# Attention and FFN of the first token group moved ahead of the loads and attention of the second, in a linear-attention kernel with a snake FFN

## The chip, the cores and the metric

The kernel runs on one core of one Trainium2 chip. The metric is device time in microseconds (us) of one execution. A run lists several executions, most of which agree within about 1.5%. The profile is one execution; its span is about 2 us below the time of the same execution. Engines are written PE (TensorE matmul), PEld (TensorE weight load), DVE (VectorE), ACT (ScalarE), POOL (GpSimd) and SP (SyncE, which issues most DMAs). Some matmul records are missing from a trace, a few per cent; the weight loads of the FFN are all there (384 for FFN1, 400 for FFN2), so work is counted by them here.

## The reference

```python
# linear attention with decay, blocks of 64, state kv per (batch, head); q, k, v: [4, 8, 768, 64]
intra = einsum(q_b, k_b) * Dmask ; intra = einsum(intra, v_b)
inter = einsum(q_b * lam_pow, kv_state)
out   = intra + inter
kv_state = lam_block * kv_state + einsum(k_b * rev_pow, v_b)
# then, on x = attention output as [3072, 512]:
h = x @ w_in                          # 512 -> 2048
s = sin(alpha * h)
g = h + s * s / (alpha + 1e-9)
y = g @ w_out                         # 2048 -> 512
```

## The kernel before

Work is cut into 24 attention *units* (256 positions of one batch and four heads) and 6 token *groups* of 512 tokens; group g needs units 4g to 4g+3. The code and the profile count groups from 0; this text says "group one" for g = 0 and "group two" for g = 1. FFN1 has 16 tiles per group (four 128x128x512 matmuls each); FFN2 has four accumulations per group (16 matmuls each).

A unit's loads are three DMAs of 256 KB on the SP queue. The weights are cast from fp32 to bf16 by DMAs that GpSimd issues:

```python
def load(u, after=None):
    for nm, src in (("q", q), ("k", k), ("v", v)):
        ld = nc.sync.dma_start(out=..., in_=...)         # 256 KB; waits for `after` if given
def load_w_in(j):  nc.gpsimd.dma_start(out=w_in_sb[..j..], in_=moe_w_in[..j..])    # 4 chunks
def load_w_out(j): nc.gpsimd.dma_start(out=w_out_sb[..j..], in_=moe_w_out[..j..])  # 4 chunks
```

A unit is scaled (QL, KD), transposed (QT), multiplied to scores, masked, and gives its state; its output needs the state before it:

```python
scores(n)            # PE into PSUM s0, s1
domask(n)            # DVE, frees s0, s1
kvmm(n, okv)         # PE
kv_copy(n, okv)      # ACT
kv_decay(n, 0)       # POOL: add, multiply, multiply (kvx, kvbd, kvs)
intermm, outmm, outev  # PE, PE, ACT: output of the unit before
```

An FFN1 tile holds one PSUM buffer from its first matmul to the end of `gall`:

```python
def fin():                                            # after the four matmuls
    s1 = sin(alpha * hps)                             # ACT
    s2 = s1 * s1                                      # on `sq`: DVE, ACT or POOL
    gall[g][:, f] = s2 * r + hps                      # DVE, then the PSUM buffer is free
```

The order of the kernel before, cut:

```python
for u in range(8): load(u)
busy(N0)                                   # filler matmuls
group(0); group(1)                         # attention of units 0..7; w_in is issued from unit 5 on (WIN0 = 5)
for f in range(16):                        # FFN1 of group one
    run(ffn1(0, f)) ; if f < 4: load_w_out(f)
    if f == GATE: load(8, after=...)       # GATE = 0
# then pairs: two FFN1 tiles of group two, two quarters of FFN2 of group one, with units 8.. between
# steady state: FFN1 tile, FFN2 quarter, alternating, one attention unit per eight of them
```

Of the kernel before, what the change touches and what calls it, by code (L numbers as in the profile page):

```python
# [12 lines left out]
BF16 = mybir.dt.bfloat16  # L13
# [4 lines left out]
def kernel(  # L18
# [23 lines left out]
    NU = 4 * NG  # L42
    RING = 8
    WIN0 = 5
    GATE = 0
# [54 lines left out]
    for u in range(8):  # L100
        load(u)
# [83 lines left out]
    def transposes(u, tag="s0", split=False):  # L185
        QT = work.tile([P, 2, 2, 2, P], BF16, name="QT")
        if split:
            pts = [ps.tile([P, 2, 2, P], BF16, name="pt", tag=tag, bufs=BUFS[tag])
                   for j in range(2)]
        else:  # L190
            pt = ps.tile([P, 2, 2, 2, P], BF16, name="pt", tag=tag, bufs=BUFS[tag])
            pts = [pt[:, 0], pt[:, 1]]
# [236 lines left out]
    def group(g, tag):  # L429

        n0 = 4 * g
        okv = None
        for n in range(n0, n0 + 4):
            nxt = n + 1 < 8
            if nxt:
                scale_q(n + 1, V)
                scale_k(n + 1, G)
            if n >= WIN0 and n < WIN0 + WCH:
                load_w_in(n - WIN0)
            okv = new_okv()  # L440
            if n > 0:
                intermm(n - 1, okv)
                outmm(n - 1, okv)
            scores(n)
            domask(n)
            kvmm(n, okv)
            kv_copy(n, okv)
            kv_decay(n, 0)
            if n > 0:
                outev(n - 1, okv)  # L450
            if nxt:
                transposes(n + 1, tag, True)
                cast_v(n + 1, A)
            busy(NB)

# [5 lines left out]
    group(0, "hps")  # L461
# [4 lines left out]
    group(1, "hps")  # L466
    for j in range(8 - WIN0, WCH):
        load_w_in(j)
    okv = new_okv()
    intermm(7, okv)  # L470
    outmm(7, okv)
    outev(7, okv)
# [4 lines left out]


    TAGS = ("hps", "s0", "hps", "s1", "hps", "ops")
    SQ = (V, A, V, A, G, A, V, G)  # L480
    for f in range(NFC):
        run(ffn1(*f1q.pop(0), SQ[f % 8], TAGS[f % 6] if f < 15 else "hps"))
        if f < 4:
            load_w_out(f)
        if f == GATE:
            load(8, after=f1mm[0, f])

    def slot(n, out=True):

        okv = new_okv()  # L490
        if out:
            intermm(n - 1, okv)
        if n < NU:
            scores(n)
        if out:
            outmm(n - 1, okv)
        if n < NU:
            kvmm(n, okv)
        if out:
            outev(n - 1, okv)  # L500
        if n < NU:
            domask(n)
            kv_copy(n, okv)
            kv_decay(n, 0)

    def dec(k):
        for _ in range(k):
            if decq and decq[0] in kva:
                kv_decay(decq.pop(0), 1)

    def macro(at, order="12121212", sq=(V,)):


        F1 = [ffn1(*f1q.pop(0), sq[i % len(sq)])
              for i in range(order.count("1")) if f1q]
        F2 = blocks(ffn2(*f2q.pop(0), "hps" if not F1 and len(f2q) % 2 else "ops"), 4)
        for j, x in enumerate(order):
            for do in at.get(j, ()):
                do()
            if x == "1":  # L520
                if F1:
                    run(F1.pop(0))
            else:
                run(F2.pop(0))

    L = lambda f, *a, **k: (lambda: f(*a, **k))


    Fa = blocks(ffn2(*f2q.pop(0)), 4)
    Fb = blocks(ffn2(*f2q.pop(0), "s1"), 4)  # L530

    def pair(k, sq):
        for j in range(2):
            run(ffn1(*f1q.pop(0), sq[j], ("hps", "s0")[j] if k < 3 else "hps"))
        run(Fa[k])
        run(Fb[k])

    scale(8, G, G, A)
    transposes_dma(8)
    pair(0, (V, A))  # L540
    load(9, after=f1mm[1, 1])
    dec(1)
    pair(1, (V, V))
    load(10)
    dec(1)
    pair(2, (V, V))
    scale(9, V, G, A)
    transposes_dma(9)
    load(11)
    pair(3, (V, V))  # L550
    dec(1)
    scale(10, V, G, A)
    transposes_dma(10)
    load(12)
    macro({1: [L(slot, 8, False)],
           3: [L(scale, 11, V, G, A), L(transposes_dma, 11), L(load, 13)],
           5: [L(slot, 9)],
           7: [L(dec, 1)]})
    macro({0: [L(scale, 12, V, G, A), L(transposes_dma, 12), L(load, 14)],
           1: [L(slot, 10)],  # L560
           5: [L(slot, 11)],
           6: [L(scale, 13, G, G, A), L(load, 15)],
           7: [L(dec, 1)]})

    for n in range(12, NU + 8):
        at = {}
        if n <= NU:
            at[0] = [L(slot, n)]
            if n + 1 < NU:
                at[0].append(L(transposes_dma, n + 1))  # L570
            if n + 2 < NU:
                at[0].append(L(scale_q, n + 2, G))
            if 16 <= n + 4 < NU:
                at[0].append(L(load, n + 4))
            at[1] = [L(dec, 2 if n < 17 else 1)]
            if n + 2 < NU:
                at[1] += [L(scale_k, n + 2, G), L(cast_v, n + 2, G)]
        if len(f2q) == 1:
            break
        macro(at, "21212121" if n % 4 == 0 else "11121222" if n == NU + 3 else "12121212")  # L580
# [30 lines left out]
```

## Time and profile before

| | before |
|---|---|
| time, median of the runs beside the changed kernel | 228.82 us (228.03 to 231.39) |
| span of the profiled execution | 227.1 us |
| first FFN1 matmul | 33.0 us |
| last matmul ends | 223.2 us |

The first view is the busy time by stretch of the FFN1 line alone. The columns are the stretch, its length, the busy time of matmuls and of weight loads with their counts, the granted clock, the DMA share and GB/s. The second stretch ends where the 193rd weight load begins, the first of FFN1 tile 49 (48 tiles are done).

```profile
core 0: us, PE busy (x) PEld busy (x), PEclk, DMA share, GB/s
0.00:33.00 33.00, 0.00 (x0) 0.00 (x0) 0.95 0.93 221
33.00:119.00 86.00, 46.07 (x186) 18.55 (x193) 0.98 0.97 197
119.00:223.30 104.30, 48.26 (x184) 18.24 (x192) 1.00 0.40 91
```

No FFN work at all is done in the first 33 us, while the DMA engines move 221 GB/s. The last stretch is TensorE at its pace; these are pieces of its chain of waits (start, length, what):

```profile
135.20 0.86 PE ops L377 x4
136.06 0.86 PE hps L349 x4
...
143.13 0.86 PE ops L377 x4
```

Four matmuls take 0.86 us, 0.216 us each before rounding; 32 of them and one attention unit repeat every 7.93 us (143.13 - 135.20), so a unit takes 7.93 - 32 x 0.216 = 1.02 us of TensorE. With these two numbers the waiting in any stretch can be worked out. From 33.0 to 119.0 us TensorE needed 192 + 132 FFN matmuls (70.0 us) and nine units (9.2 us), 79.2 of 86.0 us: about 6.8 us were lost.

The last view is the DMA queues in two stretches of 4 us, 28 to 32 and 40 to 44 us. The columns are packets, MB written, and the time of the packets as a share of 16 engines (packets overlap in the trace, so it can pass 100%, as the 105.5% below). The queue q0 carries the weights, q1 the unit loads.

```profile
q0 software_dynamic: 675, 0.67, 105.5%
```

```profile
q0 software_dynamic: 577, 0.57, 84.1%
q1 hardware_dynamic: 581, 0.29, 35.5%
```

Alone, the weights move 0.17 MB/us (of bf16; the reads are twice that: of the 27.28 MB that the page has as read from HBM, 18.87 are q, k and v, and 8.4 are left for the 4.19 MB that q0 wrote). With loads beside them they keep 0.143 and the loads get 0.073. Both queues moved the same number of packets (577 and 581); a packet of the weights is about 1.0 KB, one of the loads 0.5 KB, and that is the split of two to one.

### The profile page before, as it was taken

The page shows a single profiled execution, that of the slowest core. Times are in us where ns is not written, and L with a number is a line of the kernel's source. Part 1 is how long each engine was busy: PE and PEld are TensorE (multiplying, and loading weights), DVE is VectorE, ACT ScalarE, POOL GpSimd, SP SyncE. Part 2 cuts the span into 40 slices and gives each one's busy share as a digit, 9 for nine tenths or more (in the row PEclk, how much of TensorE's full clock was granted, in tenths as well). Part 3 has the DMA queues.
Part 4 walks back from the last instruction along what each step waited for, and adds up shares of the span by engine and source line. Part 5 has one row for each costly group of instructions (what it writes and reads, how often), then busy time and mean ns, then how long its engine had stood idle before and what let it go on. Part 6 is the DMA issues. An engine that isn't in the chain of part 4 may idle for free.

```text
span 227.1 us, 5244 instructions
## 1 busy us (share of the span) xinstructions
PE 207.8 (91%) x2054; PEld 108.9 (48%) x2077; DVE 158.3 (70%) x268; ACT 115.7 (51%) x200; POOL 114.0 (50%) x176
## 2 busy tenths in 40 slices
PE   8777679997997779999999999999999999999993
PEld 5465444433444345554554555455455444444452
DVE  3866756988895486798887998867987747667000
ACT  2463659964645345645554554445455535554121
POOL 5665995275635459999999855742611000000000
PEclk9996999999999969999999999999999999999999
DMA  5999599999769999984877777484233022201424
GB/s 149 293 289 274 139 177 185 216 213 168 227 166 171 243 204 299 200 207 95 210 158 173 153 190 180 102 208 62 56 73 68 0 49 46 46 9 40 92 49 92
DMA packets 63849, 33.92 MB, mean 149 GB/s; under 512 B 19648, under 2 KB 60880, under 8 KB 63824
## 3 DMA queue, kind: packets, MB, share of 16 engines
q1 hardware_dynamic: 59488, 29.31, 56.7%
q0 software_dynamic: 4224, 4.19, 11.4%
q8 instruction: 16, 0.26, 0.5%
q10 hardware_dynamic: 112, 0.07, 0.1%
q14 instruction: 9, 0.07, 0.1%
HBM read 27.28 MB, written 6.29 MB: 148 GB/s over the span
## 4 chain that ended last, share of the span: by engine, by line
PE 67%; DMA 11%; SPq 6%; DVE 5%; POOL 4%; issue 2%; ACT 2%; ACTq 0%; POOLq 0%
PE ops L377 32%; PE hps L349 26%; DMA st_v<-in_v_dram 8%; SPq L80 5%; DMA st_k<-in_k_dram 3%; PE sp L226 2%; DVE gall L363 2%; PE okv L320 2%; PE okv L305 2%; POOL KD L169 2%; SPq L209 1%; PE okv L254 1%; DVE QL L160 1%; PE bz L427 1%; PE pt L196 1%
## 5 line engine op out<-in xcount | busy, mean ns | idle before, releaser
L349 PE MATMUL hps<-xt,w_in_sb 128*128 128x512 bf16 x370 | 94.3, 379 | 2.4 <-DVE gall L363 1.5
L377 PE MATMUL ops<-w_out_sb,gall 128*128 128x512 bf16 (+1 forms) x391 | 94.7, 372 | 1.1 <-issue 0.7
L377 PEld LDWEIGHTS <-gall 128*128 128x128 bf16 x400 | 38.7, 98 | 42.9 <-issue 0.5
L349 PEld LDWEIGHTS <-w_in_sb 128*128 128x128 bf16 x384 | 36.8, 98 | 45.8 <-issue 3.0
L169 POOL TENSOR_TENSOR KD<-st_k,R 128x512 bf16<-128x512 f32 x24 | 27.5, 1144 | 13.0 <-DMA st_k<-in_k_dram 8.9
L237 DVE TENSOR_TENSOR ST<-sp,mask 128x512 bf16<-128x512 f32 x48 | 30.8, 683 | 3.3 <-PE sp L226 3.1
L384 ACT COPY ob<-ops 128x512 f32<-128x512 f32 (+1 forms) x25 | 14.2, 569 | 16.3 <-PE ops L377 16.3
L331 ACT CAST xt<-okv 128x512 bf16<-128x512 f32 x24 | 14.1, 586 | 6.7 <-PE okv L254 5.8
L178 ACT CAST VB<-st_v 128x512 bf16<-128x512 f32 x14 | 8.7, 623 | 14.8 <-DMA st_v<-in_v_dram 14.8
L160 POOL TENSOR_TENSOR QL<-st_q,E 128x512 bf16<-128x512 f32 x12 | 12.8, 1070 | 0.0
L427 PE MATMUL bz<-zeros 128*128 128x256 bf16 x60 | 10.6, 332 | 1.1 <-DVE warm L94 1.1
L226 PE MATMUL sp<-QT 64*64 64x128 bf16 x384 | 10.4, 228 | 1.2 <-ACT QT L200 0.7
L160 DVE TENSOR_TENSOR QL<-st_q,E 128x512 bf16<-128x512 f32 x12 | 8.7, 728 | 2.2 <-DMA st_q<-in_q_dram 2.1
L320 PE MATMUL okv<-ST,VB 64*64 64x128 bf16 x384 | 10.2, 226 | 0.0
L226 PEld LDWEIGHTS <-QT 64*64 64x64 bf16 x384 | 6.8, 111 | 3.6 <-issue 0.9
L427 PEld LDWEIGHTS <-zeros 128*128 128x128 bf16 x60 | 6.7, 119 | 2.7 <-DVE warm L94 1.1
L254 PE MATMUL okv<-VB,KD 64*64 64x64 bf16 x320 | 7.4, 198 | 0.1
L320 PEld LDWEIGHTS <-VB 64*64 64x64 bf16 x384 | 7.0, 111 | 1.0 <-issue 0.2
L180 POOL CAST VB<-st_v 128x512 bf16<-128x512 f32 x10 | 6.8, 683 | 0.0
L200 ACT COPY QT<-pt 128x512 bf16<-128x512 bf16 x8 | 4.7, 590 | 3.8 <-issue 1.7
L254 PEld LDWEIGHTS <-KD 64*64 64x64 bf16 x320 | 6.2, 114 | 0.4 <-issue 0.2
L196 PE MATMUL pt<-iden,KD 128*128 128x128 bf16 x32 | 3.4, 232 | 2.9 <-POOL KD L169 2.8
(530 smaller groups left out, 303.7 us busy)
## 6 DMA issues: line engine op xcount, KB each, us to landing
st_q<-in_q_dram SPq DMA_DIRECT2D x24, 256.0 KB, 3.6
st_k<-in_k_dram SPq DMA_DIRECT2D x24, 256.0 KB, 4.1
st_v<-in_v_dram SPq DMA_DIRECT2D x24, 256.0 KB, 4.4
out_dram<-ob SPq DMA_DIRECT2D x46, 128.0 KB, 2.5
w_in_sb<-in_moe_w_in_dram POOLq DMA_DIRECT2D x4, 512.0 KB, 6.6
w_out_sb<-in_moe_w_out_dram POOLq DMA_DIRECT2D x4, 512.0 KB, 15.3
QT<-QL SPq DMA_TRANSPOSE x16, 3.4
QT<-KD SPq DMA_TRANSPOSE x16, 2.6
```

The costliest lines, as they stand in the source:

```text
L80: ld = nc.sync.dma_start(out=tl[:].rearrange("p h two e -> p h (two e)"), in_=src[b, hh * HH:(hh + 1) * HH, tp * W:(tp + 1) * W, :] .rearr ...
L160: eng.tensor_tensor(out=QL[:], in0=stage[u][0][:].rearrange("p h two e -> p two h e"), in1=E[:, :, hs].unsqueeze(3).to_broadcast([P, 2, HH ...
L169: eng.tensor_tensor(out=KD[:], in0=stage[u][1][:].rearrange("p h two e -> p two h e"), in1=R[:, :, hs].unsqueeze(3).to_broadcast([P, 2, HH ...
L226: nc.tensor.matmul(out=sp[hd][half[c], par, hp, :], lhsT=QT[half[hd], 1, par, hp, half[c]], rhs=QT[half[hd], 0, :, hp, half[c]], start=Tru ...
L237: nc.vector.tensor_tensor(out=ST[:, hd], in0=sp[hd][:], in1=mask[:].unsqueeze(2).to_broadcast([P, 2, 2, P]), op=ALU.mult)
L254: nc.tensor.matmul(out=okv[half[hd], c, 2 * P + hp * D:2 * P + (hp + 1) * D], lhsT=KD[half[c], par, h, :], rhs=VB[half[c], par, h, :], sta ...
L320: nc.tensor.matmul(out=okv[half[hd], c, hp * P:(hp + 1) * P], lhsT=VB[half[c], par, 2 * hp + hd, :], rhs=ST[half[c], hd, par, hp, :], star ...
L331: nc.scalar.copy(out=xt[g][:, 2 * hh:2 * hh + 2, bb, :, :].rearrange("p hp c i -> p c hp i"), in_=okv[:, :, 0:2 * P].rearrange("p c (hp i) ...
L349: f1mm[g, f] = nc.tensor.matmul(out=hps, lhsT=w_in_sb[:, c, f * P:(f + 1) * P], rhs=xt[g][:, c].rearrange("p b c i -> p (b c i)"), start=( ...
L377: f2mm[:] = [nc.tensor.matmul(out=ops[:], lhsT=gall[g][:, f, m * P:(m + 1) * P], rhs=w_out_sb[:, f, col], start=(f == 0), stop=(f == NFC - ...
L384: nc.scalar.copy(out=ob[:], in_=ops[:])
L427: nc.tensor.matmul(out=bz[:], lhsT=zeros[:, :P], rhs=zeros[:], start=True, stop=True)
```

## The change

The intent: only units 0 to 3 are loaded and computed before FFN1 of group one, w_in is issued from unit 1 on, and w_out right after. The loads of units 4 to 11 wait for FFN1 tile 9 and so are issued after both weights. Units 4 to 7 run between the quarters of FFN2 of group one, whose four accumulations are all open and advance by chunk of w_out. FFN1 of group two then runs as 16 tiles in a row, with units 8 and 9 inside.

In the cut below, `B(j, m, ...)` runs quarter j of the FFN2 accumulations m; `tr` transposes a unit on TensorE, `att_s` runs its scores and state, `att_o` its output, and `att_so` the scores of one unit with the output of the unit before. `dec` runs the second, late state decay of a unit on GpSimd. `seq` runs a string of FFN1 tiles (1) and FFN2 quarters (2) and puts work before the position named: `slot` is an attention unit, `prep` scales a unit, transposes it by DMA and loads the unit four later.

```diff
-    WIN0 = 5
-    GATE = 0
+    GATE = 9
-    for u in range(8):
+    for u in range(4):
         load(u)
 ...
+    for n in range(4):
+        if n < 3: sqk(n + 1)                      # scale q on DVE, k on POOL
+        if n in (1, 2): load_w_in(n - 1)
+        attend(n, new_okv(), n - 1 if n else None)
+        ...
+    attend(None, new_okv(), 3, False)
+    load_w_in(2); load_w_in(3)
+    for j in range(WCH): load_w_out(j)
 ...
+    SQ0 = (V, A, V, A, V, A, G, V, G, A, V, G, G, V, G, G)
     for f in range(NFC):
-        run(ffn1(*f1q.pop(0), SQ[f % 8], TAGS[f % 6] if f < 15 else "hps"))
-        if f < 4: load_w_out(f)
-        if f == GATE: load(8, after=f1mm[0, f])
+        run(ffn1(*f1q.pop(0), SQ0[f], TAGS[f % 6] if f < 14 else "hps"))
+        if f == GATE:
+            for u in range(4, 8): load(u, after=f1mm[0, f] if u == 4 else None)
+            for u in range(8, 12): load(u)
 ...
+    scale(4, V, V, A)
+    B(0, 0, 1, 2, 3)                              # quarter 0 of accumulations 0..3
+    tr(4); scale(5, V, V, A)
+    B(1, 0); att_s(4); dec(1); B(1, 1, 2, 3)
+    ...                                           # the same for units 5, 6 with quarters 2, 3
+    att_so(6); dec(2); B(3, 1, 2, 3)
+    tr(7); scale(8, V, G, A); transposes_dma(8); load(12)
+    busy(NB); att_so(7); busy(NB); att_o(7)
+    SQ1 = (G, V, G, A)                            # who squares, by tile
+    seq("1" * 16, {2: [L(slot, 8, False), L(prep, 9, V, G, A), L(dec, 1)],
+                   8: [L(slot, 9), L(dec, 1), L(prep, 10, V, G, A)],
+                   14: [L(prep, 11, V, G, A)]}, SQ1, TAGS[:1])   # three PSUM buffers
+    seq("2" * 8, {1: [L(slot, 10), L(dec, 1), L(prep, 12, V, G, A)],
+                  5: [L(slot, 11), L(dec, 1), L(prep, 13, V, G, A)]}, SQ1, tags2=("ops", "hps"))
+    seq("112112112112" * 2, ...units 12 to 16...)
+    ...then "12121212" twelve times, and the rest of FFN2
```

More of the change, by code (lines that the diff above doesn't have):

```diff
@@ L187, in transposes @@
         if split:
-            pts = [ps.tile([P, 2, 2, P], BF16, name="pt", tag=tag, bufs=BUFS[tag])
+            tags = (tag, tag) if isinstance(tag, str) else tag
+            pts = [ps.tile([P, 2, 2, P], BF16, name="pt", tag=tags[j], bufs=BUFS[tags[j]])
                    for j in range(2)]
@@ L427, in busy, with sqk, attend @@
                 nc.tensor.matmul(out=bz[:], lhsT=zeros[:, :P], rhs=zeros[:], start=True, stop=True)
-    def group(g, tag):
-        n0 = 4 * g
-        okv = None
-        for n in range(n0, n0 + 4):
-            nxt = n + 1 < 8
-            if nxt:
-                scale_q(n + 1, V)
-                scale_k(n + 1, G)
-            if n >= WIN0 and n < WIN0 + WCH:
-                load_w_in(n - WIN0)
-            okv = new_okv()
-            if n > 0:
-                intermm(n - 1, okv)
-                outmm(n - 1, okv)
+    def sqk(u):
+        scale_q(u, V)
+        scale_k(u, G)
+    def attend(n, okv, n_out, with_scores=True):
+        if n_out is not None:
+            intermm(n_out, okv)
+            outmm(n_out, okv)
+        if with_scores:
             scores(n)
@@ L448, in group @@
             kv_decay(n, 0)
-            if n > 0:
-                outev(n - 1, okv)
-            if nxt:
-                transposes(n + 1, tag, True)
-                cast_v(n + 1, A)
-            busy(NB)
+        if n_out is not None:
+            outev(n_out, okv)
     busy(N0)
@@ L460 @@
     LHP, LBD = decay_tables()
-    group(0, "hps")
     ap = ps.tile([P, NFC], FP32, name="ap", tag="ops", bufs=1)
@@ L465 @@
     nc.vector.reciprocal(out=r_sb[:], in_=alpha_sb[:])
-    group(1, "hps")
-    for j in range(8 - WIN0, WCH):
-        load_w_in(j)
-    okv = new_okv()
-    intermm(7, okv)
-    outmm(7, okv)
-    outev(7, okv)
+    for n in range(4):
+        if n < 3:
+            sqk(n + 1)
+        if n in (1, 2):
+            load_w_in(n - 1)
+        attend(n, new_okv(), n - 1 if n else None)
+        if n < 3:
+            transposes(n + 1, "hps", True)
+            cast_v(n + 1, A)
+        busy(NB)
+    attend(None, new_okv(), 3, False)
+    load_w_in(2)
+    load_w_in(3)
+    for j in range(WCH):
+        load_w_out(j)
     f1q = [(g, f) for g in range(NG) for f in range(NFC)]
@@ L476, with dec, tr, att_s @@
     decq = list(range(NU))
+    def dec(k):
+        for _ in range(k):
+            if decq and decq[0] in kva:
+                kv_decay(decq.pop(0), 1)
     TAGS = ("hps", "s0", "hps", "s1", "hps", "ops")
-    SQ = (V, A, V, A, G, A, V, G)
+    SQ0 = (V, A, V, A, V, A, G, V, G, A, V, G, G, V, G, G)
     for f in range(NFC):
-        run(ffn1(*f1q.pop(0), SQ[f % 8], TAGS[f % 6] if f < 15 else "hps"))
-        if f < 4:
-            load_w_out(f)
+        run(ffn1(*f1q.pop(0), SQ0[f], TAGS[f % 6] if f < 14 else "hps"))
         if f == GATE:
-            load(8, after=f1mm[0, f])
+            for u in range(4, 8):
+                load(u, after=f1mm[0, f] if u == 4 else None)
+            for u in range(8, 12):
+                load(u)
+    def tr(u):
+        transposes(u, ("s0", "s1"), True)
+    F2 = [[] for _ in range(4)]
+    for m in range(4):
+        st = ffn2(*f2q.pop(0), ("hps", "hps", "hps", "ops")[m])
+        F2[m] = blocks(st, 4)
+    def att_s(n):
+        okv = new_okv()
+        attend(n, okv, None)
+    def att_so(n):
+        okv = new_okv()
+        attend(n, okv, n - 1)
+    def att_o(n):
+        attend(None, new_okv(), n, False)
+    def B(j, *ms):
+        for m in ms:
+            run(F2[m][j])
+    scale(4, V, V, A)
+    B(0, 0, 1, 2, 3)
+    tr(4)
+    scale(5, V, V, A)
+    B(1, 0)
+    att_s(4)
+    dec(1)
+    B(1, 1, 2, 3)
+    tr(5)
+    scale(6, V, V, A)
+    B(2, 0)
+    att_so(5)
+    dec(1)
+    B(2, 1, 2, 3)
+    tr(6)
+    scale(7, V, V, A)
+    B(3, 0)
+    att_so(6)
+    dec(2)
+    B(3, 1, 2, 3)
+    tr(7)
+    scale(8, V, G, A)
+    transposes_dma(8)
+    load(12)
+    busy(NB)
+    att_so(7)
+    busy(NB)
+    att_o(7)
     def slot(n, out=True):
@@ L504, in slot, with prep, seq @@
             kv_decay(n, 0)
-    def dec(k):
-        for _ in range(k):
-            if decq and decq[0] in kva:
-                kv_decay(decq.pop(0), 1)
-    def macro(at, order="12121212", sq=(V,)):
-        F1 = [ffn1(*f1q.pop(0), sq[i % len(sq)])
-              for i in range(order.count("1")) if f1q]
-        F2 = blocks(ffn2(*f2q.pop(0), "hps" if not F1 and len(f2q) % 2 else "ops"), 4)
+    L = lambda f, *a, **k: (lambda: f(*a, **k))
+    def prep(u, *eng):
+        scale(u, *eng)
+        transposes_dma(u)
+        if u + 4 < NU:
+            load(u + 4)
+    def seq(order, at, sq, tags1=("hps",), tags2=("ops",)):
+        n1, n2 = order.count("1"), order.count("2")
+        F1 = [ffn1(*f1q.pop(0), sq[i % len(sq)], tags1[i % len(tags1)]) for i in range(n1)]
+        F2 = []
+        for i in range(n2 // 4):
+            F2 += blocks(ffn2(*f2q.pop(0), tags2[i % len(tags2)]), 4)
         for j, x in enumerate(order):
@@ L519, in macro @@
                 do()
-            if x == "1":
-                if F1:
-                    run(F1.pop(0))
-            else:
-                run(F2.pop(0))
-    L = lambda f, *a, **k: (lambda: f(*a, **k))
-    Fa = blocks(ffn2(*f2q.pop(0)), 4)
-    Fb = blocks(ffn2(*f2q.pop(0), "s1"), 4)
-    def pair(k, sq):
-        for j in range(2):
-            run(ffn1(*f1q.pop(0), sq[j], ("hps", "s0")[j] if k < 3 else "hps"))
-        run(Fa[k])
-        run(Fb[k])
-    scale(8, G, G, A)
-    transposes_dma(8)
@@ L540 @@
-    pair(0, (V, A))
-    load(9, after=f1mm[1, 1])
-    dec(1)
-    pair(1, (V, V))
-    load(10)
-    dec(1)
-    pair(2, (V, V))
-    scale(9, V, G, A)
-    transposes_dma(9)
-    load(11)
-    pair(3, (V, V))
-    dec(1)
-    scale(10, V, G, A)
-    transposes_dma(10)
-    load(12)
-    macro({1: [L(slot, 8, False)],
-           3: [L(scale, 11, V, G, A), L(transposes_dma, 11), L(load, 13)],
-           5: [L(slot, 9)],
-           7: [L(dec, 1)]})
-    macro({0: [L(scale, 12, V, G, A), L(transposes_dma, 12), L(load, 14)],
-           1: [L(slot, 10)],
-           5: [L(slot, 11)],
-           6: [L(scale, 13, G, G, A), L(load, 15)],
-           7: [L(dec, 1)]})
@@ L565 @@
-    for n in range(12, NU + 8):
+            run((F1 if x == "1" else F2).pop(0))
+    SQ1 = (G, V, G, A)
[4 more added lines that the diff above has]
+                  5: [L(slot, 11), L(dec, 1), L(prep, 13, V, G, A)]}, SQ1, tags2=("ops", "hps"))
+    seq("112112112112" * 2,
+        {0: [L(slot, 12), L(dec, 1), L(prep, 14, G, G, A)],
+         5: [L(slot, 13), L(dec, 1), L(prep, 15, G, G, A)],
+         10: [L(slot, 14), L(dec, 1), L(prep, 16, G, G, A)],
+         15: [L(slot, 15), L(dec, 1), L(prep, 17, G, G, A)],
+         20: [L(slot, 16), L(dec, 1), L(prep, 18, G, G, A)]}, (V, V, A, V))
@@ L566 @@
+    for i in range(12):
         at = {}
+        n = 17 + i
         if n <= NU:
-            at[0] = [L(slot, n)]
-            if n + 1 < NU:
-                at[0].append(L(transposes_dma, n + 1))
+            at[1] = [L(slot, n), L(dec, 2)]
             if n + 2 < NU:
-                at[0].append(L(scale_q, n + 2, G))
-            if 16 <= n + 4 < NU:
-                at[0].append(L(load, n + 4))
-            at[1] = [L(dec, 2 if n < 17 else 1)]
-            if n + 2 < NU:
-                at[1] += [L(scale_k, n + 2, G), L(cast_v, n + 2, G)]
@@ L578 @@
-        if len(f2q) == 1:
-            break
-        macro(at, "21212121" if n % 4 == 0 else "11121222" if n == NU + 3 else "12121212")
+                at[1].append(L(prep, n + 2, G, G, G))
+        seq("12121212", at, (V,))
+    for m in range(3):
+        run(ffn2(*f2q.pop(0), "hps" if m % 2 else "ops"))
     run(ffn2(*f2q[0], "ops", slice(0, DM // 2)))
```

## The prediction

> **What bounds the kernel now.** Two stages. From 84 us to the end the chain of waits is TensorE alone: FFN matmuls of 0.216 us (four in 0.864), one attention unit per 7.93 us period, so a unit costs TensorE 7.93 - 32 x 0.216 = 1.02 us. From 33 us the needed TensorE work is 768 x 0.216 = 165.9 us plus 17 units, 183.2 us; the last matmul ends at 223.2 us, so only 7 us is lost after 33 us (timeline: gaps at 52, 56, 72 and 79 us). The first 33 us hold no FFN matmul (stretches of the FFN1 line): eight attention units, one per 2.7 us, run behind 6.3 MB of loads at 285 GB/s, and w_in is issued only at 25 us. The change attacks that head.
>
> **What the change does.** Four units instead of eight precede FFN1; w_in is issued from about 12 us. Before, unit 3's scores were at 16.6 us; now two weight issues (0.8-0.95 us) sit on GpSimd inside the loop. I estimate FFN1 to start at 19.8 us, 13.2 us earlier. Four units (4 x 1.02, and 4 x 0.45 of transposes) move behind it: about 190 us of work. Without any new stall the span would be 19.8 + 190 + 4 = 214.
>
> **New stalls, estimated from traced durations.**
> 1. DMA. Weights alone moved 0.17 MB/us (bf16 written); with loads beside them (40 to 48 us) 0.143, loads 0.073 (DMA view by stretch). [...] So unit 4, gated at FFN1 tile 9 (28 us), lands at 37-40 us, unit 5 at 43-44, w_out at 42. FFN2 of group one reaches unit 4 at 38 us; unit 5's scaling stands on VectorE before unit 4's mask. Loss 3-4 us.
> 2. Hand-over from FFN1 to FFN2, 1 us, and the exposed unit 7 after FFN2, 3 us.
> 3. FFN1 of group two runs as 16 tiles without FFN2 between. VectorE needs 16 x 0.75 + 4 x 0.42 + two masks (2 x 1.29) + three scalings (0.69) = 18.4 us against TensorE's 15.9. Worse, tiles 2 and 8 have their square (1.03 us) on GpSimd behind two decays of 1.46 us and one k scaling of 1.1 us. With three PSUM buffers each costs up to 4 us. Loss 3-8 us. VectorE squares also stretch from 0.42 to 1.24 us beside GpSimd[...].
> 4. The 16 FFN1 with 8 FFN2 quarters: VectorE 5.3 us per five blocks and a slot against TensorE's 5.34: 0-2 us.
>
> The head's 13 us lie fully on the critical path; new losses of 10-18 us replace the old 7. Added in full they give a span near 229; such waits partly overlap, and the hand-set engine lists suggest balancing, so I expect 224.5 span, 226.5 us (times are 2 us above the span).
>
> **Prediction:** 226.5 us, 219 to 234 in 8 of 10; faster by over 2% 0.40, within 2% 0.38, slower 0.22.
>
> **What would show the steps.** First FFN1 matmul at 19-21 us; FFN1 of group one gapless for 14 us; waits of QL and KD for loads of units 4 and 5 at 38-45 us; gaps in FFN1 of group two at tiles 5 and 11, ended by gall; after about 92 us saturated TensorE at 0.216 us.
>
> **What would make it wrong.** Weights later than 20 us; loads keeping less than a third of the DMA beside w_out; GpSimd blocking FFN1 of group two less or more than estimated; a lower granted clock.

VectorE squares in the trace of the kernel before took 0.42 us with no GpSimd instruction beside them and up to 1.24 us with one; the cause was not shown. The sum: 19.8 + 190 + 4 = 214 us without new stalls; the stalls 3-4, 1 + 3, 3-8 and 0-2 us are the 10-18 us; in full that gave a span near 229 us, of which 4.5 were taken off, 224.5, and 226.5 us with the 2 us between time and span.

## The result, and the profile after

| | before | after |
|---|---|---|
| time, median | 228.82 us (228.03 to 231.39) | 248.51 us (246.25 to 249.5) |
| ratio after / before, 95% interval | | 1.0883 (1.0806 to 1.0960) |
| span of the profiled execution | 227.1 us | 247.4 us |
| first FFN1 matmul | 33.0 us | 20.2 us |
| last matmul ends | 223.2 us | 243.5 us |

Ratios are the mean time of one kernel's fast runs over that of the other's of the same rounds, so not quite the ratio of the medians. The same view of the FFN1 line of the changed kernel:

```profile
core 0: us, PE busy (x) PEld busy (x), PEclk, DMA share, GB/s
0.00:20.19 20.19, 0.00 (x0) 0.01 (x1) 0.92 0.94 203
20.19:136.40 116.21, 48.35 (x184) 19.14 (x193) 0.91 0.86 182
136.40:243.60 107.20, 49.00 (x190) 18.78 (x192) 1.00 0.35 79
```

This is the whole ledger. The head is 12.8 us shorter (33.0 to 20.2). The middle, to the same FFN1 tile (49, a point of equal FFN1 work in both kernels), is 30.2 us longer (86.0 to 116.2). The rest is 2.9 us longer (104.2 to 107.1 by the end of the last matmul), of which 0.9 us are four FFN2 matmuls that the middle had not done. The sum is the 20.3 us between the spans. The steady pace is untouched, as two pieces of the chain of waits show:

```profile
139.97 0.86 PE hps L349 x4
140.83 0.86 PE ops L377 x4
```

The middle now needs 192 + 128 FFN matmuls (69.1 us), 13 units (13.3 us), four units' transposes (an estimate of 0.45 us each, as four of the eight take some 0.4 us and overlap) and eight fillers (0.109 us each, by their starts in the trace at full clock, 0.9 us), 85.1 us. So 5.9 us of its 30.2 us is work that moved in, and the waits in it went from 6.8 to 31.1 us. Where they are, the busy time of all engines by stage shows. The stages are FFN1 of group one (20.2 to 35), FFN2 of group one with units 4 to 7 (35 to 67.5), FFN1 of group two (67.5 to 97.2), two accumulations of FFN2 (97.2 to 109.7), and the mixed stage:

```profile
core 0: us, PE busy (x) PEld busy (x) DVE busy (x) ACT busy (x) POOL busy (x), PEclk, DMA share, GB/s
20.20:35.00 14.80, 13.70 (x65) 6.16 (x64) 11.26 (x18) 12.47 (x20) 8.46 (x10) 1.00 1.13 178
35.00:67.50 32.50, 24.18 (x303) 13.51 (x304) 15.85 (x26) 10.72 (x21) 12.94 (x23) 0.85 1.10 252
67.50:97.20 29.70, 20.09 (x149) 8.50 (x149) 15.77 (x24) 14.68 (x25) 16.86 (x22) 0.82 0.40 102
97.20:109.70 12.50, 10.03 (x188) 5.78 (x188) 7.29 (x11) 5.41 (x11) 9.11 (x15) 1.00 0.68 131
109.70:139.40 29.70, 27.11 (x353) 14.41 (x348) 24.82 (x40) 21.68 (x39) 26.15 (x40) 1.00 1.01 210
```

| stage | length | TensorE needs | lost |
|---|---|---|---|
| FFN1 of group one | 14.8 | 13.8 | 1.0 |
| FFN2 of group one, units 4 to 7 | 32.5 | 13.8 + 4.1 + 1.8 + 0.9 = 20.6 | 11.9 |
| FFN1 of group two, units 8, 9 | 29.7 | 13.8 + 2.0 = 15.8 | 13.9 |
| two FFN2 accumulations, units 10, 11 | 12.5 | 6.9 + 2.0 = 8.9 | 3.6 |

In the two bad stages no engine is full: VectorE is busy 15.8 of 29.7 us, ScalarE 14.7, GpSimd 16.9. This is waiting along chains, not a lack of throughput. Also, the granted clock is 0.85 and 0.82 there.

What TensorE waited for in these two stages (the view of waits; the columns are who waited for whom, us in total, how often, the longest), first 35 to 67.5 us, then 67.5 to 97.2 us:

```profile
PE bz L427 <- ACT ob L384: 4.0, 1, 4.0
PE pt L196 <- DVE KD L168: 1.9, 1, 1.9
```

```profile
PE hps L349 <- DVE gall L363: 9.2, 5, 4.9
```

The 9.2 us are waits for a PSUM buffer. The timeline shows what held it, at the first of the two long ones (start, length, engine, line, what, and in brackets the engine's idle time before it and what ended it):

```profile
72.50 1.04 POOL L168 TENSOR_TENSOR KD<-st_k,R 128x512 bf16<-128x512 f32 x1
73.50 0.45 POOL L285 TENSOR_TENSOR kvx<-kva,kvs 128x128 f32<-128x128 f32 x1
74.03 0.61 POOL L288 TENSOR_TENSOR kvbd<-kvx,LBD 128x256 bf16<-128x256 f32 x1
74.60 0.85 POOL L293 TENSOR_TENSOR kvs<-kvx,LHP 128x128 f32<-128x128 f32 x1
75.41 2.03 POOL L362 TENSOR_TENSOR s<-s 128x512 bf16<-128x512 bf16 x2
76.48 2.06 DVE L363 SCALAR_TENSOR_TENSOR gall<-s,r_sb,hps 128x512 bf16<-128x512 bf16 x3 [1.29 <-POOL s L362]
77.28 2.28 PE L349 MATMUL hps<-xt,w_in_sb 128*128 128x512 bf16 x7 [3.14 <-DVE gall L363]
```

GpSimd took its instructions in program order here. Tile 2's square (75.41) stands behind a k scaling and a late decay; the sine that it squares had ended at 71.90 us, 3.5 us earlier. `gall` of that tile waits for the square, the PSUM buffer for `gall`, and TensorE for the buffer, 3.14 us. The other long one, before 90.27 us, is of the same kind and lasts 4.9 us.

The other wait, of 4.0 us, goes through the SP queue. This is the timeline of SP and of ScalarE there:

```profile
56.51 0.78 SPq L79 DMA_DIRECT2D st_v<-in_v_dram  x1
57.39 6.70 SPq L389 DMA_DIRECT2D out_dram<-ob  x8
64.19 1.32 SPq L209 DMA_TRANSPOSE QT<-QL  x1
```

```profile
62.38 0.59 ACT L384 COPY ob<-ops 128x512 f32<-128x512 f32 x1 [4.07 <-DMA out_dram<-ob]
```

The last load of the burst for units 4 to 11 was issued at 56.5 us. The eight stores of FFN2 of group one came behind it and took 6.7 us to issue, and unit 8's transposes came behind the stores. The fourth eviction had to wait for the first store, because there are three staging buffers; that store was issued at 57.39 us and landed at 61.95 us, just behind the last of the loads (61.59 us).

The shares of the DMA queues were as before, here from 36 to 40 us, which is why unit 4's k took 12.3 us to land (issued at 29.75, used at 42.05). The first five loads, issued beside the weights, took 8.5 to 13.2 us; those issued from 42.0 us on, after the last weight had landed (41.9 us), took 5.0 to 5.6 us where the landing is recorded:

```profile
q0 software_dynamic: 567, 0.56, 83.0%
q1 hardware_dynamic: 566, 0.28, 35.1%
```

Last, the clock, by stretches of 4 us around the two long gaps of TensorE (columns as in the stage view):

```profile
74.00:78.00 4.00, 0.86 (x5) 0.35 (x4) 2.71 (x5) 0.71 (x2) 3.41 (x4) 1.00 0.22 44
78.00:82.00 4.00, 4.00 (x22) 1.60 (x24) 1.79 (x4) 1.58 (x3) 1.04 (x1) 0.57 0.76 206
...
86.00:90.00 4.00, 0.00 (x0) 0.00 (x0) 0.53 (x1) 0.16 (x1) 3.92 (x6) 0.81 0.26 52
90.00:94.00 4.00, 3.73 (x9) 1.31 (x9) 2.50 (x5) 1.44 (x3) 0.43 (x1) 0.50 0.76 204
```

After each gap TensorE is busy again but at about half clock: 12 matmuls from 77.28 us on took 4.41 us, 0.37 us each. The clock records of this trace hold low-clock stretches of 3.4 or 6.8 us, all at 0.50. The five stretches of the changed kernel start at 9.95, 44.08, 61.15, 78.22 and 88.45 us, whole multiples of 3.41 us apart. With the trace cut into windows on this grid, from 13 to 242 us, TensorE was busy for at most 1.6 us of each window that came before half clock, and for 2.0 us or more of every other; but the window before the first stretch (6.54 to 9.95 us) was busy for 2.1 us, so no threshold is shown. A gap need not be as long as a window: one of 1.9 us, from 40.9 to 42.8 us, preceded the stretch of 44.1 to 47.5 us, and in the kernel before TensorE was busy for 0.76 of the 3 us from 78 us, and a stretch of 0.50 came from 80.5 to 83.9 us. In both the low clock fell on work that had already resumed. The stretches sum to 24 us before 100 us in the changed kernel, 20.5 us of it in the middle of the ledger, and to 6.8 and 3.4 us in the kernel before.

All lines of the view of waits, and not only those shown, sum to 8.3 us in the first bad stage and 9.5 us in the second, of 11.9 and 13.9 us lost. The other 3.6 and 4.4 us are, by this estimate, the half clock.

### The profile page after: what moved, and what is told of

The parts are those of the page before. It is cut to its first block, busy times and chain, and to the rows that moved or that the text cites. A ratio compares the mean times of both kernels' runs of the same rounds, so it can differ in the third digit from the quotient of the medians.

```text
span 247.4 us, 5236 instructions
## 1 busy us (share of the span) xinstructions
PE 213.2 (86%) x2042; PEld 110.3 (45%) x2069; DVE 154.6 (63%) x259; ACT 121.1 (49%) x210; POOL 113.5 (46%) x175
## 4 chain that ended last, share of the span: by engine, by line
PE 59%; DMA 15%; POOL 11%; ACT 4%; issue 3%; DVE 3%; SPq 3%; POOLq 0%; ACTq 0%
PE ops L377 27%; PE hps L349 24%; DMA st_k<-in_k_dram 7%; DMA QT<-KD 4%; POOL KD L168 3%; POOL kvbd L288 2%; PE sp L226 2%; SPq L79 2%; PE okv L320 2%; POOL kvs L293 2%; DVE gall L363 2%; DMA out_dram<-ob 2%; POOL kvx L285 2%; DMA st_v<-in_v_dram 1%; PE okv L305 1%
## 5 line engine op out<-in xcount | busy, mean ns | idle before, releaser
L356 ACT ACTIVATE s<-hps,alpha_sb 128x512 bf16<-128x512 f32 x96 | 65.2, 687 | 63.4 <-PE hps L349 62.3
L363 DVE SCALAR_TENSOR_TENSOR gall<-s,r_sb,hps 128x512 bf16<-128x512 bf16 x96 | 70.8, 747 | 20.9 <-POOL s L362 13.1
L349 PEld LDWEIGHTS <-w_in_sb 128*128 128x128 bf16 x384 | 37.9, 100 | 58.9 <-issue 18.3
L362 DVE TENSOR_TENSOR s<-s 128x512 bf16<-128x512 bf16 x70 | 37.4, 534 | 25.1 <-ACT s L356 24.9
L237 DVE TENSOR_TENSOR ST<-sp,mask 128x512 bf16<-128x512 f32 x48 | 30.8, 683 | 13.8 <-PE sp L226 13.6
L285 POOL TENSOR_TENSOR kvx<-kva,kvs 128x128 f32<-128x128 f32 x32 | 15.6, 487 | 30.3 <-ACT kva L268 30.2
L168 POOL TENSOR_TENSOR KD<-st_k,R 128x512 bf16<-128x512 f32 x20 | 23.2, 1161 | 2.6 <-DMA st_k<-in_k_dram 2.0
L362 POOL TENSOR_TENSOR s<-s 128x512 bf16<-128x512 bf16 x14 | 14.6, 1054 | 17.7 <-ACT s L356 14.3
L288 POOL TENSOR_TENSOR kvbd<-kvx,LBD 128x256 bf16<-128x256 f32 x32 | 20.3, 635 | 2.5
L177 ACT CAST VB<-st_v 128x512 bf16<-128x512 f32 x19 | 11.9, 626 | 13.1 <-DMA st_v<-in_v_dram 13.1
L288 POOL TENSOR_TENSOR kvbd<-kva,LBD 128x256 bf16<-128x256 f32 x8 | 4.9, 616 | 19.8 <-ACT kva L268 19.7
L293 POOL TENSOR_TENSOR kvs<-kvx,LHP 128x128 f32<-128x128 f32 x24 | 12.1, 504 | 0.0
L268 ACT COPY kva<-okv 128x256 f32<-128x256 f32 (+1 forms) x24 | 8.2, 340 | 5.5 <-PE okv L254 5.5
## 6 DMA issues: line engine op xcount, KB each, us to landing
w_out_sb<-in_moe_w_out_dram POOLq DMA_DIRECT2D x4, 512.0 KB, 13.8
```

The source lines that it names most:

```text
L168: eng.tensor_tensor(out=KD[:], in0=stage[u][1][:].rearrange("p h two e -> p two h e"), in1=R[:, :, hs].unsqueeze(3).to_broadcast([P, 2, HH ...
L237: nc.vector.tensor_tensor(out=ST[:, hd], in0=sp[hd][:], in1=mask[:].unsqueeze(2).to_broadcast([P, 2, 2, P]), op=ALU.mult)
L285: nc.gpsimd.tensor_tensor(out=Xt[:], in0=A, in1=prev[:], op=ALU.add)
L288: nc.gpsimd.tensor_tensor(out=bd[:], in0=X.unsqueeze(2).to_broadcast([P, 2, 2, D]), in1=LM, op=ALU.mult)
L293: nc.gpsimd.tensor_tensor(out=new[:], in0=X, in1=L, op=ALU.mult)
L349: f1mm[g, f] = nc.tensor.matmul(out=hps, lhsT=w_in_sb[:, c, f * P:(f + 1) * P], rhs=xt[g][:, c].rearrange("p b c i -> p (b c i)"), start=( ...
```

## The experiments

Theories before the first experiments: (A) the squares behind slot work on GpSimd; (B) the stores behind the burst of loads; (C) unit 4's late load; and the clock as a multiplier. The rivals are that the waits only show at these places and would come back elsewhere, or that the order itself is too dear. Every kernel gave a correct result. The "middle" is the length from the first FFN1 matmul to the equal-work tile of the ledger (before 86.0 us, changed 116.2 us).

| kernel | edit to the changed kernel | median us | ratio to before (95%) | first FFN1 | middle |
|---|---|---|---|---|---|
| changed | | 248.51 | 1.0883 (1.0806-1.0960) | 20.2 | 116.2 |
| e1_square | three squares off GpSimd | 242.17 | 1.0608 (1.0540-1.0676) | 20.6 | 108.3 |
| e2_ob4 | fourth output buffer | 247.10 | 1.0869 (1.0805-1.0934) | 20.0 | 114.3 |
| e3_fill | fillers in the two gaps | 246.37 | 1.0822 (1.0755-1.0888) | 20.2 | 114.4 |
| e4_load5 | unit 4 loaded at the start | 246.97 | 1.0801 (1.0720-1.0882) | 20.6 | 112.9 |
| e5_late9 | loads of units 9-11 later | 244.97 | 1.0699 (1.0609-1.0789) | 19.6 | 115.1 |
| e6_three | e1 + e4 + e5 | 239.99 | 1.0456 (1.0392-1.0520) | 21.1 | 105.2 |
| e7_hold1 | e6, one FFN2 accumulation moved | 239.01 | 1.0403 (1.0328-1.0479) | 20.7 | 106.3 |
| e8_hold2 | e6, two moved | 239.03 | 1.0396 (1.0308-1.0484) | | |
| e9_load8 | units 0-7 loaded at the start | 246.41 | 1.0805 (1.0728-1.0882) | 21.7 | 111.4 |
| e10_load8_sq | e9 + squares off GpSimd | 237.15 | 1.0415 (1.0338-1.0492) | 21.6 | 103.1 |
| e11_load8_hold1 | e10, one accumulation moved | 235.97 | 1.0316 (1.0223-1.0409) | 21.3 | 101.9 |
| e12_load8_hold2 | e10, two moved | 235.69 | 1.0338 (1.0252-1.0425) | 21.3 | 100.7 |
| e13_tail | e12, GpSimd reordered | 234.05 | 1.0242 (1.0182-1.0303) | 21.3 | 101.3 |
| e14_buf4 | e10, fourth PSUM buffer | 239.37 | 1.0497 (1.0449-1.0545) | 22.1 | 103.7 |
| e15_win3 | *kernel before*, early w_in | 233.94 | 1.0244 (1.0189-1.0298) | 38.5 | 85.5 |

(e8_hold2's profile fell in a slow execution, so its stages are not read.)

### e1_square: the squares

```diff
-                   14: [...]}, SQ1, TAGS[:1])                 # SQ1 = (G, V, G, A)
+                   14: [...]}, (G, V, A, A, G, V, G, A, A, V, G, A, G, V, A, A), TAGS[:1])
```

> Changed kernel (247.4 us span), with only the squares of tiles 2, 8 and 14 of FFN1 of group two moved from GpSimd to ScalarE (and the one of tile 11 kept there). Theory A (GpSimd runs in order, so these squares wait behind 4 us of decays and k scaling, hold one of three PSUM buffers and stop TensorE): the gaps of 3.1 us at 74 and 4.9 us at 85 us go, and with them the halved clock of some 4 us after each; FFN1 of group two falls from 29.5 us (67.9 to 97.4) to 20-22 us and the time by 7-9 us, to about 240. Rival (this stage is bound by the sum of work on VectorE and ScalarE, the wait only shows at GpSimd): the gaps come back in other tiles, under 3 us saved.

The time fell by 2.5% (ratio 1.0883 to 1.0608), about 6.3 us where 7 to 9 was expected; the intervals do not touch. FFN1 of group two fell from 29.7 to 22.5 us (68.1 to 90.6), its granted clock rose from 0.82 to 0.97, and it was 1.00 from 74 to 90 us. The wait for `gall` in this stage is now:

```profile
PE hps L349 <- DVE gall L363: 5.5, 6, 1.8
```

The total fell from 9.2 to 5.5 us and the longest from 4.9 to 1.8. Theory A holds. Some waiting remains that the squares do not explain, so the rival is true for a part.

### e2_ob4: a fourth output buffer

```diff
-    outp = ctx.enter_context(tc.tile_pool(name="outp", bufs=3))
+    outp = ctx.enter_context(tc.tile_pool(name="outp", bufs=4))
```

> Changed kernel with four output staging buffers instead of three. Theory B (the fourth eviction of FFN2 of group one waits for the first store, which stood in the DMA queue behind the loads of units 4 to 11; 4.1 us of ScalarE wait ending at 62.4 us): the wait goes, FFN1 of group two starts at 62-63 us instead of 67.9, and the time falls by 4-6 us to 242.5-244.5. Rival (the units after it would have waited for the transposed loads and the exposed unit 7 anyway): under 2 us.

The wait did go, and FFN1 of group two started at 61.4 instead of 67.5 us. The time hardly moved (1.0869 against 1.0883, inside the intervals). The waits of TensorE between 57 and 95 us show where the 6 us went:

```profile
PE hps L349 <- DVE gall L363: 9.4, 3, 5.0
PE sp L226 <- DMA QT<-KD: 3.0, 1, 3.0
```

Unit 8's transposes stand in the same SP queue behind the same stores, so slot 8 waits 3.0 us for them. The gaps behind the squares did not shrink either: 4.2 us at tile 5 (3.1 in the changed kernel) and 5.0 at tile 11 (4.9). So the fourth buffer removed a wait and not its cause, and most of the expected gain was given back at the next waits, the first of them on that same queue. My expectation was wrong, and the rival was right.

### e3_fill: the clock

```diff
-    seq("1" * 16, {2: [...],
+    seq("1" * 16, {2: [...], 5: [L(busy, 24)], 11: [L(busy, 40)],
```

> Changed kernel with 24 and 40 filler matmuls (0.107 us each at full clock) put before tiles 5 and 11 of FFN1 of group two, inside the gaps of 3.1 and 4.9 us; nothing else. Clock theory (an idle TensorE of 3 us halves the granted clock, and the 12 and 16 matmuls after the gaps took 0.37 instead of 0.216 us for that): granted clock 1.00 between 76 and 96 us, tiles at 0.86 us, time lower by 3-4 us (243.5-244.5) although work is added. Rival (the matmuls after the gaps are slow for their inputs, or the fillers just delay): same or slower.

The same stretches of 4 us as shown of the changed kernel, with the fillers:

```profile
74.00:78.00 4.00, 3.48 (x29) 2.69 (x28) 2.71 (x4) 0.92 (x2) 3.58 (x5) 1.00 0.17 34
78.00:82.00 4.00, 3.45 (x65) 1.93 (x64) 2.62 (x6) 2.84 (x5) 1.04 (x1) 1.00 0.62 159
...
86.00:90.00 4.00, 3.78 (x31) 2.79 (x29) 1.69 (x3) 0.00 (x0) 3.23 (x4) 1.00 0.36 73
90.00:94.00 4.00, 3.00 (x13) 1.16 (x12) 2.43 (x5) 3.56 (x6) 1.81 (x2) 1.00 0.67 194
```

The clock was 1.00 in all six stretches of 4 us from 74 to 98 us, so in this stage idle time, not the inputs, is what halved it. The stage fell from 29.7 to 27.5 us. The time fell by 0.6%, about 1.4 us, with overlapping intervals: the sign is as expected, but the size is less than half of it and not clear of noise. The halved clock is therefore shown as a mechanism. Its price in this stage is about 2 us by this one profile; the estimate from the waits was 4.4 us. Part of the difference may be the fillers themselves (64 x 0.109 = 7.0 us, with 3.1 us of gaps left beside them, against 9.5 us of gaps before). Over the whole span the mean granted clock was 0.979, against 0.952 in the changed kernel.

### e4_load5 and e5_late9: the loads

```diff
# e4_load5: unit 4 with the first loads, the gate starts at unit 5
-    for u in range(4): load(u)
+    for u in range(5): load(u)
# e5_late9: the burst ends with unit 8
-            for u in range(8, 12): load(u)
+            load(8)
-    transposes_dma(8); load(12)
+    transposes_dma(8); for u in range(9, 13): load(u)
```

> Changed kernel with unit 4 loaded at the start with units 0 to 3 (0.77 MB, about 2.7 us of DMA ahead of w_in), the rest as it is. Theory C (unit 4, gated behind both weights, lands at 42 us and keeps TensorE from 40.7 to 42.8 and later): transposes of unit 4 follow the FFN2 quarter at once, the low clock of 44 to 48 us goes, time lower by 2-4 us even if FFN1 starts 0.5-1.5 us later. Rival (unit 5, still gated, is then the one waited for; the gain is given back): same within 1 us.

> Changed kernel with only the loads of units 9, 10 and 11 moved behind unit 8's transposes, three output buffers as in the changed kernel. Queue theory (loads of units 4 to 11 are one 24-deep burst on one in-order DMA queue; the output stores and unit 8's transposes stand behind it; with four output buffers the wait only moved from the stores to the transposes, 3.0 us at slot 8): both the 4 us wait for the store and the 3 us wait for the transposes go, FFN1 of group two starts at 61-62.5 us and slot 8 follows without a gap; time 240-243. Rival (the stores are slow by themselves, or the loads of 9 to 11 are then late): over 245.

With e4_load5 the wait for unit 4's KD went, and with it the half-clock stretch of 44.1 to 47.5 us (the mean granted clock of the profiled run is 0.965, that of the changed kernel 0.952); FFN1 of group two started at 65.2 us instead of 67.5, although the wait for the store grew from 4.0 to 5.0 us. The time fell by 0.75%, about 1.9 us, with overlapping intervals. With e5_late9 that stage started at 62.4 us, the 4.0 us wait for the store shrank to 0.5 us and slot 8's wait for transposes from the 3.0 us of e2_ob4 to 1.4. The time fell by 1.7%, about 4.2 us, and its 245.0 us lies short of the 240 to 243 that I expected. Queue order is a cause, then, but part of the gain was taken back. TensorE's wait for `gall` was 9.8 us in this kernel. The squares still stood on GpSimd, and unit 9's cast on ScalarE, ahead of the next tiles' sines, now waited 3.6 us for its late load, so the rival named beforehand (the loads of 9 to 11 are then late) holds for a part. This is what is left of the wait for the store:

```profile
PE bz L427 <- ACT ob L384: 0.5, 1, 0.5
```

### e6_three, e7_hold1, e8_hold2: the cures together

e6_three has the edits of e1, e4 and e5. e7_hold1 and e8_hold2 also take one or two of the four FFN2 accumulations out of the attention of units 4 to 7:

```diff
# e8_hold2 (e7_hold1 keeps three and uses "11112" * 4)
-    for m in range(4):
+    for m in range(2):
-    B(1, 1, 2, 3)
+    B(1, 1)                            # and so on for the other quarters
-    seq("1" * 16, {2: ..., 8: ..., 14: ...
+    seq("112" * 8, {3: ..., 12: ..., 21: ...
```

> The three cures together: loads of 9 to 11 late, unit 4 loaded at the start, squares of tiles 2, 8 and 14 off GpSimd. If the causes are separate and on the critical path, the savings nearly add (5 + 6 + 2 us): 233-236 us. If they hide one another: above 238. The rest over the kernel before would then be the order itself: 16 FFN1 tiles in a row need more of VectorE than of TensorE.

> As the three cures together, and the fourth FFN2 accumulation of group one (16 matmuls, 3.46 us) taken out of the attention of units 4 to 7 and spread, a quarter after every four tiles, over FFN1 of group two. If that FFN1 stage is bound by VectorE and ScalarE (22 us for 15.9 us of TensorE work), the moved matmuls are free there: 2-3.5 us less than the three cures alone. If TensorE or the buffers bound it: no change.

> The same with two of the four FFN2 accumulations of group one spread over FFN1 of group two (a quarter after every two tiles). Order theory: 4-7 us less than the three cures alone, 227-231 us, about the kernel before. Rival (units 4 to 7 with half the FFN2 work between them then wait for their loads): no better than with one held back.

The single savings (6.3 + 1.9 + 4.2 = 12.4 us by the ratios) became 9.8 us together, about four fifths of the sum. But 233 to 236 us was expected and 240 came, and by the line that I had drawn beforehand (above 238 us) the causes hide one another in part. ScalarE shows one reason, in e6_three:

```profile
67.92 0.62 ACT L177 CAST VB<-st_v 128x512 bf16<-128x512 f32 x1 [3.57 <-DMA st_v<-in_v_dram]
```

As in e5_late9, moving unit 9's load later made its cast, which stands in ScalarE's order before the next tiles' sines, wait 3.6 us for the data. TensorE then stood 4.1 us. The cure for one queue had made the next one late. Holding back FFN2 work brought less than 1.5 us here, inside the intervals, so these two do not decide on the order.

### e9_load8 to e12_load8_hold2: the load order undone

```diff
# e9_load8
-    for u in range(4): load(u)
+    for u in range(8): load(u)
-            for u in range(4, 8): load(u, after=f1mm[0, f] if u == 4 else None)
-            for u in range(8, 12): load(u)
+            for u in range(8, 12): load(u, after=f1mm[0, f] if u == 8 else None)
# e10_load8_sq, besides: squares (G, V, A, V, A, V, G, V, A, V, A, V, A, V, A, V)
# e11_load8_hold1, e12_load8_hold2, besides: as e7_hold1, e8_hold2
```

> One part of the change undone: all of units 0 to 7 are loaded at the start as in the kernel before, only units 8 to 11 wait for the gate; everything else is the changed kernel. If the load order is a main cause (units 4 and 5 late, stores and transposes behind a 24-deep burst): no wait for units 4 and 5, no 4 us wait for the store, FFN1 of group two from 67.5 to 60-62 us, time 240-242. It also tests whether w_in needs the DMA for itself: if it does, FFN1 of group one starts 2 us or more later than 20.2 us or has gaps; the shares measured beside each other (weights two thirds) say it does not. Rival (load order matters little, the stages further on do): over 245.

> As e9_load8, and in FFN1 of group two no square on GpSimd behind a slot's work there (GpSimd keeps tiles 0 and 6; the others alternate VectorE and ScalarE). If the two causes are separate: another 5-8 us, 233-236 us, the stage of 16 tiles about 21 us long. Rival (ScalarE's casts waiting for loads or VectorE fill the gap): less than 3 us more.

> As e10_load8_sq, with one of four FFN2 accumulations of group one spread over FFN1 of group two, where VectorE is short and TensorE is not. Order theory: 2-3.5 us less than e10_load8_sq. Rival: no change, as between the three cures and the first version of this.

> As e10_load8_sq, with two of four FFN2 accumulations spread over FFN1 of group two. With units 4 to 7 loaded early, half the FFN2 work may be enough to cover them: 4-7 us less than e10_load8_sq, about 228-231 us. Rival (a unit's own chain of scaling, transposes, scores and mask then shows, some 4 us each): no better than e11_load8_hold1.

Undoing the load order alone moved the time by 0.7%, inside the intervals, so I was wrong to expect 240 to 242 us. The waits for unit 4 and most of that for the store went (1.5 us were left), but FFN1 now waited for its weights:

```profile
PE hps L349 <- DMA w_in_sb<-in_moe_w_in_dram: 1.6, 1, 1.6
```

FFN1 of group one started 1.5 us later and FFN2 2.9 us later (37.9 against 35.0 us). The change's reason for the gate, that w_in needs the DMA, was right in kind.

On this base the squares were worth 3.6% (1.0805 to 1.0415, same chip, same rounds), about 8.9 us. This is more than the 6.3 us of e1_square, but the edit is larger too: it takes six squares off GpSimd (tiles 2, 4, 8, 10, 12 and 14), not three, and moves four more from ScalarE to VectorE. So it confirms that squares on GpSimd cost time, and the two sizes cannot be compared as one cause with and without the loads. Holding back one or two accumulations brought the ratio to 1.0316 and 1.0338. The size is 1.8 to 2.3 us by the ratios, with overlapping intervals, less than the 4 to 7 us expected of two. In e12_load8_hold2 the FFN1 stage is well filled (TensorE busy 24.15 of 24.5 us), but units 4 to 7 with half the FFN2 work between them took 20.3 us for an estimated 13.7 us of TensorE work (the 20.6 us above less two accumulations of 3.46 us). The wait went from one stage to the other.

### e13_tail, e14_buf4, e15_win3: what is left

```diff
# e13_tail, to e12_load8_hold2
-        st = ffn2(*f2q.pop(0), ("hps", "hps", "hps", "ops")[m])
+        st = ffn2(*f2q.pop(0), ("ops", "hps")[m])
-    att_so(6); dec(2)
+    att_so(6)                          # dec(2) goes behind att_o(7)
-    scale(8, V, G, A)
+    scale(8, V, V, A)
-    ... L(dec, 1), L(prep, 12, V, G, A) ...
+    ... L(prep, 12, V, G, A), L(dec, 1) ...      # the same for units 10 and 13 to 18
# e14_buf4, to e10_load8_sq
-    ... TAGS[:1])
+    ... ("hps", "hps", "hps", "ops"))
# e15_win3, to the kernel BEFORE
-    WIN0 = 5
+    WIN0 = 3
```

> As e12_load8_hold2, with GpSimd's work put in another order and no work removed: the two late decays after unit 6 come after unit 7's output, unit 8's k scaling goes to VectorE, in the slots the scaling of the next unit comes before the late decay; and the first FFN2 accumulator is the free one, so that FFN2 of group one need not wait for the last FFN1 evictions. If GpSimd's order is what exposes unit 7 (3.0 us wait of TensorE for the decayed state at 53.8 us) and makes the transposes late (4.5 us of waits for them): 5-8 us less, 228-231 us. Rival (TensorE then waits for VectorE or ScalarE instead): less than 2 us.

> As e10_load8_sq, with a fourth PSUM buffer in FFN1 of group two. There TensorE waited 5.1 us for gall in five places, the stage took 23.8 us for 15.9 us of matmuls. If the buffers are too few: stage 20-21 us, 2-4 us less time. If VectorE and ScalarE are simply full (about 20 us of work each by the traced durations): less than 1.5 us.

> The kernel before, with w_in issued two units earlier (from about 17 us instead of 25 us) and nothing else: early weights alone, on the old order. If early weights are what the head needs: FFN1 starts earlier than 33.0 us and the time falls by 1-3 us. If the head is the eight units' own chain, and weights beside loads take two thirds of the DMA: FFN1 starts at 33-36 us and the time is the same or up to 3 us more.

e13_tail cut TensorE's wait for the decayed state from 3.0 to 0.7 us, and the middle stayed as it was (101.3 against 100.7 us): 2.3 us came back as a wait for unit 8's transposes and 2.1 us as a wait for QL.

```profile
PE sp L226 <- DMA QT<-KD: 2.3, 1, 2.3
PE pt L196 <- DVE QL L159: 2.1, 1, 2.1
```

The time is the best of all variants, 1.0242 ("unclear" by the 2% rule, its interval begins at 1.0182), but it overlaps the interval of e12_load8_hold2, so GpSimd's order, as changed here, was not what held the rest.

e14_buf4 made FFN1 of group two shorter, from 23.8 to 20.4 us, as expected if buffers were short. But the next stage paid it back, growing from 12.0 to 15.1 us, because FFN2 then waited for the same `gall`. These are its waits from 36 to 100 us:

```profile
PE ops L377 <- DVE gall L363: 4.6, 3, 3.1
PE hps L349 <- DVE gall L363: 3.3, 6, 1.3
```

Both stages together take 35.5 us against 35.8, for an estimated 24.8 us of TensorE work. The buffer moved the wait and did not remove it. The time was no better (1.0497 against 1.0415; two different chips).

e15_win3 is the early weights alone, on the old order, and it is slower by 2.4%. Its middle (85.5 us) and its rest (104.2 us) are those of the kernel before; only the first FFN1 matmul moved, from 33.0 to 38.5 us. GpSimd waited 8.4 us for loads between 15 and 40 us:

```profile
POOL KD L169 <- DMA st_k<-in_k_dram: 8.4, 3, 6.0
```

The weights took the DMA from units that were still needed. Its verdict by the 2% rule is "unclear", because the interval reaches just below 2%, but it is clear of no change.

## Why the prediction was wrong

The prediction said 226.5 us, with a range of 219 to 234 and 0.22 for slower. The time was 248.5 us. The head came as said. What failed is the sum of new stalls behind it: 10 to 18 us were put down and 31.1 us were lost. The terms for units 4 to 7 (7 to 8 us put down, 11.9 lost) and for FFN1 of group two (3 to 8 put down, 13.9 lost) were too small, because the shared SP queue and the half clock that came with each gap were left out, and the FFN2 accumulations after them had no term (3.6 lost).

- **Right: the head.** FFN1 was to start at 19.8 us and started at 20.2; FFN1 of group one was to be gapless for 14 us and took 14.8, with 13.7 us busy. The moved work was foreseen too (190 us from there without stalls).
- **Right in place, too small in size: FFN1 of group two.** "With three PSUM buffers each costs up to 4 us. Loss 3-8 us." The gaps came at tiles 5 and 11, ended by `gall`, of 3.1 and 4.9 us, as described. But the stage lost 13.9 us. The step that failed is that I counted a gap as its length only. With each of these gaps came a time at half clock (0.50); two stretches of 3.4 and 6.8 us lie in this stage (e3_fill shows the cause, and a price of about 2 us; the estimate from the waits is 4.4). The prediction named a lower granted clock among what would make it wrong, but put nothing down for it. And further waits for `gall` remained after the squares were gone (5.5 us in e1_square). Moving three squares brought 6.3 us, and moving six, on e9_load8, 8.9 us.
- **Wrong: units 4 to 7.** The prediction had 3-4 us for the loads, 1 us for the hand-over and 3 us for exposed unit 7. The stage lost 11.9 us. The DMA part was about right in kind (k of unit 4 landed at 42.0 us where 37-40 was said; TensorE waited 1.9 us). What was missing is that stores and transposes use the same SP queue as the burst of 24 loads: 4.0 us for the store, and 3.0 us behind it for the transposes once the first was cured (e2_ob4). A half-clock stretch of 6.8 us came with it (0.50 from 61.15 to 67.97 us).
- **Missed: the two FFN2 accumulations after it** lost 3.6 us, 2.2 of it in waits for the DMA transposes of units 10 and 11; nothing was put down for them.
- **Wrong direction: the discount.** "Such waits partly overlap, and the hand-set engine lists suggest balancing, so I expect 224.5." In full my own terms gave 229; I took 4.5 us off, of the 22.9 us by which the span was missed (247.4 against 224.5). In the runs, waits removed one at a time did mask one another (e2_ob4, e13_tail, e14_buf4), but in the kernel as it was they stood one after the other and the clock was lower besides (mean 0.952, against 0.985 in the kernel before). The kernel before lost 6.8 us in the middle and the changed one 31.1, where 10-18 us was put down against 7.
- **Right: the steady state** at 0.216 us per matmul came back. The pieces shown are at 139 us, but of the 31.1 us lost only 0.7 fall after 109.7 us, so the pace was nearly there at about 110 us, where the prediction had 92.

Why no repaired version beat the kernel before: the best, e13_tail, starts FFN1 11.7 us earlier (21.3 against 33.0), but its middle is 15.3 us longer (101.3 against 86.0) and its end 2.4 us (106.6 against 104.2). Of the 15.3 us, 5.9 us is worked out to be the moved work (four units, which before ran while the loads came in, in time that TensorE could not use otherwise). So the 12.8 us at the head were never worth more than about 7. The other 9.4 us are waits and half clock that the repairs left; in the last ones (e13_tail, e14_buf4) what was taken from one place came back at another.

What stays open: whether another order of units 4 to 7 could hide them. The runs show that neither the PSUM buffers (e14_buf4) nor the change of GpSimd's order (e13_tail) nor the amount of FFN2 work between the units (e7, e8, e11, e12) alone decides it. The common form, just-in-time items on several in-order queues, is argued from their traces and not shown by a run that removes it.

## What to carry to other kernels

Work that runs while the loads come in can be free, as units 4 to 7 were here (moved, they cost 5.9 us of TensorE by the ledger); before moving it behind the start of the main work, subtract its time there from the gain at the head. GpSimd, ScalarE and the SP queue took their items in program order in these traces (a square began 3.5 us after its input was there, and in e6_three a cast waited 3.6 us for its load and the sine behind it came after it). Where that is so, ask of every small item (a square, a cast, a store, a transpose) what stands ahead of it; taking away one wait pays only if the next item on the same queue is not waiting for the same thing, as the fourth output buffer showed (a start 6 us earlier, of which the time kept 0.3). When a stall of a few us on TensorE is predicted, put down a half-clock stretch with it: here the two longest, of 4.0 and 4.9 us, each came with one of 6.8 us, and those of 1.9 and 3.1 us each with one of 3.4 us.
